# The four products of a column block of w_out with phi, emitted as one group of four strips

## The chip, the cores and the metric

The kernel runs on one core of one Trainium2 chip. The metric is device microseconds (us) of one execution of the whole program. Before the change the median of 3 runs is 520.47 us, the lowest 518.27 and the highest 520.8.

## The reference

A chain of an attention read, a gated feed-forward layer and a soft mixture of experts. Cut to what matters here:

```python
# x [8, 8, 512, 64], state [8, 8, 32, 64]; attn_out: reads of state by x and of x by state
x = attn_out.transpose(0, 2, 1, 3).reshape(8 * 544, 512)
h = x @ w_in                                   # w_in [512, 2048], held in float64
g = where(h >= 1, h, where(h <= -1, 0, (h + 1) ** 2 / 4))
x = g @ w_out                                  # w_out [2048, 512], held in float64
logits = x @ phi                               # phi [512, 32]
d = softmax of logits over the tokens; c = softmax of logits over the slots
slot_input = d.T @ x
# eight experts: relu(slot_input[e] @ w1[e]) @ w2[e]  -> slot_out
out = c @ slot_out
```

## The kernel before, in words

The feed-forward output x = g @ w_out is never formed. The kernel forms the small matrix wp = w_out @ phi (2048 by 32) once, and for each batch b = 0..7 (512 tokens each, and a ninth round for the state rows) the logits E = g @ wp. The sum d.T @ g is kept over the batches in `acc`, and multiplied by w_out only at the end.

**Conversion.** w_in and w_out lie in memory as 64-bit floats. `convert` (L155 to L171) turns a piece of 128 partitions by 512 numbers into 32-bit floats by bit operations: two on VectorE (L159, L161), and then either one more on VectorE (L164), or two on ScalarE through `act` (L133) and one on VectorE (L171). `piece` (L173) picks the one or the other by the list `CFG["conv"]`.

**w_out.** `conv_wo(i)`, i = 8..15, treats half of a block g = 0..3 of 512 rows of w_out, which lie as columns (w_out is loaded transposed): two pieces k of 128 of the 512 inner numbers each. For each piece it converts into `cw_w[k]`, which is a quarter of the tile `acc`; multiplies it by phi into the strip of partitions 32k to 32k+31 of the PSUM tile `wps[g]` (L195: the stationary operand is phi's 128 by 32, the moving one 128 by 512); turns it back by four transposes on TensorE (L198, tile `wtp`); and copies the result to `wD` on ScalarE. Behind the second half, `wD` goes to memory (L202), `wps` is copied to `wsb` on ScalarE (L204), four small products with a constant (L207) add the four strips and turn them, and ScalarE copies the result to `wp` (L208). The pool psE of `wps` has one buffer, so a block's first product waits until the block before it has been copied out at L208. `cw_w[k]` has one buffer too: the next block's piece k, whose first instruction is L159, waits until the product and the transposes that read it are done.

**Where it stands.** In the loop over b and over m = 0..15 (a step m is one `hstep`, 128 of the 2048 columns of h), `CFG["todo"]` puts the conversions into round b = 0: block 0 ahead of step m = 7, block 1 at m = 10, block 2 at m = 11, block 3 at m = 12 and 13. Each `hstep` is six products (L445; for the first four steps two, L436), two or three passes on ScalarE and GpSimd, and one on VectorE (L497). `vchunk` (tile `V`, L376) makes a quarter of the state side of h for a round: eight products side by side, then ScalarE, then a subtraction on VectorE (L395). `attention(b + 1)` runs beside it.

**What sets the order.** The program is written in this order, but up to round 2 the compiler's list scheduler places the instructions of each engine: it goes by the order in which they were emitted and by its own estimate of when operands are ready. From round 2 TensorE runs in the written order. Each engine runs its own queue in order. The helper `group` (L122) emits products that are to run side by side: the first one can be told to wait for a list of instructions, and the rest are raised in priority and ordered behind the first:

```python
first = mm(**calls[0])
for i in after:
    tc.add_manual_dep(first.ins, i.ins.name, SYNC, reason="side by side")
with tc.high_priority(CFG["hp"]):
    for c in calls[1:]:
```

It records its first product at L124 and the others at L129; `estep` (tile `E`) uses it for four strips of the same shape as those of L195.

Of the kernel before, what the change touches and what calls it, by code (L numbers as in the profile page):

```python
# [11 lines left out]
ALU = mybir.AluOpType  # L12
# [9 lines left out]
def kernel(  # L22
# [14 lines left out]
    nc = tc.nc  # L37
# [25 lines left out]
    phi_t = const.tile([128, 4, 32], F32, name="phi_t")  # L63
# [53 lines left out]
    mm = nc.tensor.matmul  # L117
# [4 lines left out]
    def group(calls, after=()):  # L122
# [6 lines that stand above are left out]
                e = mm(**c)  # L129
                tc.add_manual_dep(e.ins, first.ins.name, ORDER, reason="side by side")  # L130

    def act(out, in_, func=ACTF.Copy, **kw):
        return nc.scalar.activation(out=out, in_=in_, func=func, **kw)  # L133


    stage = [wb_s[0], wb_s[1], a_st, nat_s[3], gD_s[0], gD_s[1]] * 2 + [wb_s[0], wb_s[1], gD_s[0], gD_s[1]]
    cw_w = [acc[:, 512 * i:512 * i + 512] for i in range(4)]
# [3 lines left out]
    def stage_load(i):  # L141
        if i >= 16:
            return
        src = win[i // 2, :, 1024 * (i % 2):1024 * (i % 2) + 1024] if i < 8 else wout[i - 8]
        dma(out=stage[i].bitcast(U32), in_=src.bitcast(U32))
# [5 lines left out]
    def nxt(i):  # L151
        later = [j for j in range(i + 1, 16) if stage[j] is stage[i]]
        return later[0] if later else 16

    def convert(src, dst, tmp):  # L155

        w = src.bitcast(U32).rearrange("p (f w) -> p f w", w=2)
        lo, hi, d = w[:, :, 0], w[:, :, 1], dst.bitcast(U32)
        nc.vector.tensor_scalar(out=d, in0=hi, scalar1=0x07FFFFFF, scalar2=3,  # L159
                                op0=ALU.bitwise_and, op1=ALU.logical_shift_left)  # L160
        nc.vector.scalar_tensor_tensor(out=d, in0=hi, scalar=0xC0000000, in1=d,  # L161
                                       op0=ALU.bitwise_and, op1=ALU.bitwise_or)
        if tmp is None:
            nc.vector.scalar_tensor_tensor(out=d, in0=lo, scalar=29, in1=d,  # L164
                                           op0=ALU.logical_shift_right, op1=ALU.bitwise_or)
        else:
            t = tmp.bitcast(U32)

            act(tmp, lo, ACTF.Relu, scale=-2.0 ** -29, bias=seven)
            act(t, tmp, ACTF.Relu, scale=-1.0, bias=seven)  # L170
            nc.vector.tensor_tensor(out=d, in0=d, in1=t, op=ALU.bitwise_or)  # L171

    def piece(i, k, dst):  # L173
        rot["t"] += 1
        tmp = None if rot["t"] in CFG["conv"] else cw_t[rot["t"] % 3]
        convert(stage[i][:, 1024 * k:1024 * k + 1024], dst, tmp)

    def conv_win(i):
        c, h = divmod(i, 2)
        for k in range(2):  # L180
            piece(i, k, win_t[c][:, 2 * h + k, :])
        stage_load(nxt(i))

    wps, wD = {}, {}

    def conv_wo(i):

        g, h = divmod(i - 8, 2)
        if h == 0:
            wps[g] = psE.tile([128, 512], F32, tag="E", name="wps")  # L190
            wD[g] = rot_g.tile([128, 4, 512], F32, tag="g", name="wD")
        for k in range(2 * h, 2 * h + 2):
            w = cw_w[k]
            piece(i, k % 2, w)
            mm(out=wps[g][32 * k:32 * k + 32, :], lhsT=phi_t[:, k, :], rhs=w, start=True, stop=True)  # L195
            tp = psX.tile([128, 4, 128], F32, tag="X", name="wtp")
            for x in range(4):
                nc.tensor.transpose(tp[:, x, :], w[:, 128 * x:128 * x + 128], ident)  # L198
            act(wD[g][:, :, 128 * k:128 * k + 128], tp)
        stage_load(nxt(i))  # L200
        if h == 1:
            dma(out=wo32[g], in_=wD[g].rearrange("p x d -> p (x d)"))  # L202
            sb = rot_q.tile([128, 512], F32, tag="q", name="wsb")
            act(sb, wps[g])  # L204
            wpp = wps[g][:, 0:128].rearrange("p (x n) -> p x n", x=4)
            for x in range(4):
                mm(out=wpp[:, x, :], lhsT=sb[:, 128 * x:128 * x + 128], rhs=R4, start=True, stop=True)  # L207
            act(wp[:, 4 * g:4 * g + 4, :], wpp)  # L208
# [587 lines left out]
    drain(v0)  # L796
    drain(a0)
    todo = [lambda i=i: conv_win(i) for i in range(2, 8)] + [lambda i=i: conv_wo(i) for i in range(8, 16)]

    sm = None  # L800
    vg = None
    order = ExitStack()
    for b in range(B + 1):
# [11 lines left out]
        for m in range(NM):  # L815
# [9 lines left out]
            if b > 0 and m % 4 == 0:  # L825
                k = 4 * b + m // 4 - 2
# [102 lines left out]
    for i in range(4):  # L929
        for jj in range(4):  # L930
            mm(out=SI[32 * jj:32 * jj + 32, :], lhsT=PT[:, jj, 32 * i:32 * i + 32],
               rhs=where["wo", i][1][jj], start=(i == 0), stop=(i == 3))
# [13 lines left out]
    for i in range(16):  # L946
        e, hf = divmod(i, 2)
        place, w = where["w1", i]
        for kt in range(4):
            mm(out=h1[hf][32 * kt:32 * kt + 32, :], lhsT=XD[e // 4][:, kt, 32 * (e % 4):32 * (e % 4) + 32], rhs=w[kt],  # L950
               start=(e == 0), stop=(e == 7))
# [134 lines left out]
```

## Time and profile before

| | us |
|---|---|
| median of 3 runs | 520.47 |
| profiled execution | 520.69 |
| its span, first to last instruction | 518.5 |
| PE busy (matmul) | 462.9 |
| DVE busy | 369.0 |
| ACT busy | 313.4 |
| POOL busy | 209.5 |

PE is TensorE, PEld its weight loads, DVE is VectorE, ACT is ScalarE, POOL is GpSimd, SP issues DMAs. Every float32 product leaves two matmul records, so the 16 products of L195 are counted as 32. In a list in order of time, a row gives start, length, engine, line, operation, tiles (output <- input), and how many records are merged into it; in brackets stands how long the engine was idle before it and what ended that. Lengths overlap a little, since an instruction is counted until its last result is written; the distance from start to start is what an instruction takes from its engine.

### The profile page before, as it was taken

The numbers are of one execution on the slowest core, as the hardware profiler recorded it, in microseconds if no ns is written. First come the engines' busy times: TensorE is split into PE (matmuls) and PEld (weight loads), VectorE is DVE, ScalarE is ACT, GpSimd is POOL, SyncE is SP. The second block draws the span as 40 slices with busy tenths as digits, with TensorE's granted clock in tenths as the row PEclk, the third lists the DMA queues.
The fourth block names the chain that finished last, engine by engine and source line by source line (L and its number), as shares of the span: only waits on it lengthen the run. The fifth ranks groups of instructions, "written<-read, shape, count | busy, mean of one in ns | idle before, by whom it ended". The sixth has DMA issues, their size and how long they took to land.

```text
span 518.5 us, 9979 instructions
## 1 busy us (share of the span) xinstructions
PE 462.9 (89%) x3757; PEld 267.5 (52%) x3757; DVE 369.0 (71%) x768; ACT 313.4 (60%) x613; POOL 209.5 (40%) x211
## 2 busy tenths in 40 slices
PE   5382999999989999999998998999999769799994
PEld 2130465566545555555565455556457548335583
DVE  2999798869568879969968987985896745310370
ACT  0778997677667667767766866866656426211242
POOL 0000000045527776776776776877573100110041
PEclk9685999999999999999999999999999979989965
DMA  8998072546449797697596877789589898899998
GB/s 314 420 419 362 6 317 84 164 163 181 145 163 332 268 292 247 205 322 253 197 314 201 283 265 239 274 284 336 185 277 353 322 398 323 301 385 418 385 298 292
DMA packets 40127, 142.39 MB, mean 275 GB/s; under 512 B 3984, under 2 KB 12560, under 8 KB 27920
## 3 DMA queue, kind: packets, MB, share of 16 engines
q1 hardware_dynamic: 38400, 133.91, 72.5%
q0 software_dynamic: 1680, 7.87, 4.4%
q8 instruction: 29, 0.48, 0.4%
q14 instruction: 18, 0.15, 0.1%
HBM read 100.34 MB, written 41.42 MB: 273 GB/s over the span
## 4 chain that ended last, share of the span: by engine, by line
PE 62%; DVE 11%; DMA 7%; POOL 7%; issue 6%; ACT 5%; SPq 1%; ACTq 0%; POOLq 0%
PE h L445 24%; DMA gdr<-gD 5%; POOL v L393 4%; PE E L124 4%; PE V L124 4%; PE F L124 3%; PE h L950 3%; POOL c L475 3%; PE ops L129 3%; PE h L453 3%; PE wps L195 2%; DVE g L497 2%; ACT c L133 2%; PE gtp L523 2%; PE wtp L198 2%
## 5 line engine op out<-in xcount | busy, mean ns | idle before, releaser
L445 PE MATMUL h<-a,v 128*128 128x512 f32 x744 | 192.4, 403 | 7.1 <-DVE g L497 7.0
L445 PEld LDWEIGHTS h<-a,v 128*128 128x128 f32 x744 | 133.6, 188 | 71.2 <-DVE g L497 20.0
L475 POOL TENSOR_TENSOR c<-c 128x512 f32<-128x512 f32 x84 | 87.1, 1043 | 118.4 <-ACT c L133 117.7
L133 ACT ACTIVATE c<-h,half 128x512 f32<-128x512 f32 x128 | 87.9, 688 | 47.8 <-PE h L445 29.6
L497 DVE SCALAR_TENSOR_TENSOR g<-h,c 128x512 f32<-128x512 f32 x112 | 74.7, 671 | 36.3 <-POOL c L475 30.3
L393 POOL TENSOR_TENSOR v<-vc,v 128x512 fp32r<-128x512 f32 x48 | 61.9, 1290 | 49.6 <-ACT vc L133 49.4
L534 DVE STREAM_TRANSPOSE gD<-g 128x512 f32<-128x512 f32 x108 | 74.9, 700 | 1.8
L133 ACT ACTIVATE v<-V 128x512 fp32r<-128x512 f32 x62 | 37.1, 598 | 11.9 <-PE V L129 10.6
L124 PE MATMUL V<-win,st_t 64*32 64x512 f32 x64 | 35.9, 643 | 6.8 <-ACT att L133 5.5
L129 PE MATMUL V<-win,st_t 64*32 64x512 f32 x448 | 39.1, 636 | 0.0
L133 ACT ACTIVATE vc<-V 128x512 f32<-128x512 f32 x48 | 28.6, 596 | 15.0 <-POOL v L393 15.0
L124 PE MATMUL F<-nat,dN 128*32 128x512 f32 x54 | 26.6, 614 | 7.0 <-DMA nat<-gdr 6.6
L129 PE MATMUL E<-g,wp 128*32 128x512 f32 x168 | 29.6, 605 | 0.0
L124 PE MATMUL E<-g,wp 128*32 128x512 f32 x56 | 29.3, 605 | 0.0
L133 ACT ACTIVATE c<-c 128x512 f32<-128x512 f32 x44 | 27.8, 632 | 0.7
L129 PE MATMUL F<-nat,dN 128*32 128x512 f32 x162 | 26.8, 615 | 0.0
L453 PE MATMUL h<-XSh,v 128*128 128x256 f32 x128 | 26.1, 294 | 0.2 <-ACT nat L133 0.2
L641 DVE SCALAR_TENSOR_TENSOR acc<-acc,al,F 128x512 f32<-128x512 f32 x28 | 19.4, 724 | 7.3 <-PE F L129 7.3
L453 PEld LDWEIGHTS h<-XSh,v 128*128 128x128 f32 x128 | 20.7, 192 | 4.9 <-issue 1.7
L1036 POOL DMA_DIRECT2D out_dram<-o x16 | 7.9, 500 | 36.3 <-DVE o L1004 30.2
L129 PE MATMUL ops<-so,LC 32*128 32x256 f32 x160 | 20.6, 371 | 0.9 <-ACT o L133 0.8
L133 ACT ACTIVATE o<-ops 128x256 f32<-128x256 f32 x34 | 11.5, 381 | 15.8 <-PE ops L129 15.8
(238 smaller groups left out, 817.7 us busy)
## 6 DMA issues: line engine op xcount, KB each, us to landing
gdr<-gD SPq DMA_DIRECT2D x108, 256.0 KB, 6.8
nat<-gdr SPq DMA_DIRECT2D x27, 1024.0 KB, 6.2
w<-in_w_dram SPq DMA_DIRECT2D x24, 1024.0 KB, 10.7
xn<-in_xn_dram SPq DMA_DIRECT2D x8, 1024.0 KB, 8.6
out_dram<-o SPq DMA_DIRECT2D x16, 512.0 KB, 4.4
xs<-in_xs_dram SPq DMA_DIRECT2D x7, 1024.0 KB, 8.7
w<-in_w_dram POOLq DMA_DIRECT2D x5, 1024.0 KB, 8.9
wb<-in_win_dram SPq DMA_DIRECT2D x4, 1024.0 KB, 11.4
```

The lines of the kernel that those rows point to most:

```text
L124: first = mm(**calls[0])
L129: e = mm(**c)
L133: return nc.scalar.activation(out=out, in_=in_, func=func, **kw)
L195: mm(out=wps[g][32 * k:32 * k + 32, :], lhsT=phi_t[:, k, :], rhs=w, start=True, stop=True)
L393: nc.gpsimd.tensor_tensor(out=lo[:, G, :], in0=vf, in1=hi[:, G, :], op=ALU.subtract)
L445: mm(out=h, lhsT=v[:, G, f], rhs=a[:, G, :], start=(k == 0), stop=(k == 5))
L453: mm(out=h, lhsT=w[:, j, :], rhs=x[:, j, :], start=(k == 0), stop=(k == 11))
L475: nc.gpsimd.tensor_tensor(out=c, in0=c, in1=c, op=ALU.mult)
L497: gI[b, m] = nc.vector.scalar_tensor_tensor(out=g, in0=h, scalar=1.0, in1=c, op0=ALU.max, op1=ALU.min)
L534: nc.vector.transpose(out=gd[:, :, :, m4, :].rearrange("p c a i -> p a c i"), in_=gT[b, m].rearrange("p (a c i) -> p a c i", a=4, i=32))
L641: nc.vector.scalar_tensor_tensor(out=a, in0=a, scalar=al, in1=F, op0=ALU.mult, op1=ALU.add)
L950: mm(out=h1[hf][32 * kt:32 * kt + 32, :], lhsT=XD[e // 4][:, kt, 32 * (e % 4):32 * (e % 4) + 32], rhs=w[kt], start=(e == 0), stop=(e == 7))
```

## The change

`convert` and `piece` return the last instruction of a conversion. `conv_wo` keeps it in `cvt[k]`, no longer emits a product behind each piece, and emits the four products of a block as one `group` behind both halves, whose first product waits for the four conversions.

```diff
+            return nc.vector.scalar_tensor_tensor(out=d, in0=lo, scalar=29, in1=d, ...
+            return nc.vector.tensor_tensor(out=d, in0=d, in1=t, op=ALU.bitwise_or)
...
-        convert(stage[i][:, 1024 * k:1024 * k + 1024], dst, tmp)
+        return convert(stage[i][:, 1024 * k:1024 * k + 1024], dst, tmp)
...
-    wps, wD = {}, {}
+    wps, wD, cvt = {}, {}, {}
...
         for k in range(2 * h, 2 * h + 2):
             w = cw_w[k]
-            piece(i, k % 2, w)
-            mm(out=wps[g][32 * k:32 * k + 32, :], lhsT=phi_t[:, k, :], rhs=w, start=True, stop=True)
+            cvt[k] = piece(i, k % 2, w)
             tp = psX.tile([128, 4, 128], F32, tag="X", name="wtp")
             for x in range(4):
                 nc.tensor.transpose(tp[:, x, :], w[:, 128 * x:128 * x + 128], ident)
             act(wD[g][:, :, 128 * k:128 * k + 128], tp)
         stage_load(nxt(i))
         if h == 1:
+            group([dict(out=wps[g][32 * k:32 * k + 32, :], lhsT=phi_t[:, k, :], rhs=cw_w[k], start=True, stop=True) for k in range(4)],
+                  [cvt[k] for k in range(4)])
             dma(out=wo32[g], in_=wD[g].rearrange("p x d -> p (x d)"))
```

## Rows read from the trace of the kernel before

**Rows 1.** Busy time of each engine by stretch (us: span, engines, granted clock, DMA)
```profile
52.00:62.00 10.00, 10.00 (x50) 4.66 (x48) 6.42 (x12) 9.26 (x17) 0.00 (x0) 0.90 0.01 2
62.00:86.00 24.00, 24.00 (x158) 15.03 (x156) 23.96 (x52) 20.46 (x40) 0.00 (x0) 1.00 0.56 219
86.00:104.00 18.00, 18.00 (x158) 9.37 (x151) 13.53 (x24) 13.34 (x28) 0.00 (x0) 1.00 0.39 118
52.00:107.20 55.20, 55.20 (x383) 31.83 (x389) 43.95 (x87) 45.86 (x88) 1.10 (x2) 0.98 0.40 146
107.20:400.00 292.80, 282.93 (x2249) 160.76 (x2234) 238.37 (x471) 198.43 (x382) 194.62 (x183) 1.00 0.76 251
```

**Rows 2.** The same by stretch, of line 195 alone (PE, PEld, clock, DMA)
```profile
52.00:62.00 10.00, 2.73 (x8) 0.42 (x8) 0.90 0.01 2
62.00:86.00 24.00, 4.28 (x12) 0.56 (x10) 1.00 0.56 219
86.00:104.00 18.00, 6.28 (x14) 0.83 (x14) 1.00 0.39 118
```

**Rows 3.** PE in order of time: single products, and two at once
```profile
55.45 1.04 PE L195 MATMUL wps<-acc,phi_t 128*32 128x512 f32 x2
56.42 0.44 PE L198 MATMUL wtp<-cst_t,acc 128*128 128x128 f32 x2
...
58.40 1.04 PE L195 MATMUL wps<-acc,phi_t 128*32 128x512 f32 x2
...
61.37 1.05 PE L195 MATMUL wps<-acc,phi_t 128*32 128x512 f32 x4
```

**Rows 4.** PE in order of time: four strips of the tile E, one group
```profile
121.10 0.63 PE L129 MATMUL E<-g,wp 128*32 128x512 f32 x3
...
121.56 0.60 PE L129 MATMUL E<-g,wp 128*32 128x512 f32 x3
```

**Rows 5.** DVE in order of time: ends of blocks 0 to 2, starts of blocks 1 to 3
```profile
53.74 0.69 DVE L171 TENSOR_TENSOR acc<-acc,LT 128x512 uint32<-128x512 uint32 x1 [0.84 <-ACT LT L133]
58.61 0.42 DVE L159 TENSOR_SCALAR acc<-gD 128x512 uint32<-128x512 uint32 x1
73.03 0.68 DVE L164 SCALAR_TENSOR_TENSOR acc<-gD,acc 128x512 uint32<-128x512 uint32 x1
74.37 0.43 DVE L159 TENSOR_SCALAR acc<-wb 128x512 uint32<-128x512 uint32 x1
85.07 0.43 DVE L159 TENSOR_SCALAR acc<-gD 128x512 uint32<-128x512 uint32 x1
85.41 0.70 DVE L164 SCALAR_TENSOR_TENSOR acc<-wb,acc 128x512 uint32<-128x512 uint32 x1
```

**Rows 6.** DVE in order of time: its waits of the same stretch
```profile
61.47 0.43 DVE L159 TENSOR_SCALAR acc<-gD 128x512 uint32<-128x512 uint32 x1 [0.99 <-PE wtp L198]
86.77 0.69 DVE L497 SCALAR_TENSOR_TENSOR nat<-h,c 128x512 f32<-128x512 f32 x1 [0.67 <-ACT c L133]
90.20 0.43 DVE L159 TENSOR_SCALAR acc<-gD 128x512 uint32<-128x512 uint32 x1 [1.14 <-PE wtp L198]
93.20 0.43 DVE L159 TENSOR_SCALAR acc<-gD 128x512 uint32<-128x512 uint32 x1 [0.77 <-PE wtp L198]
102.08 0.69 DVE L395 TENSOR_TENSOR v<-V,v 128x512 fp32r<-128x512 f32 x1 [0.66 <-ACT v L133]
```

**Rows 7.** PE in order of time: last products of blocks 2 and 3, first step of round 1
```profile
90.09 1.05 PE L195 MATMUL wps<-acc,phi_t 128*32 128x512 f32 x2
102.68 1.05 PE L195 MATMUL wps<-acc,phi_t 128*32 128x512 f32 x2
104.51 1.62 PE L445 MATMUL h<-a,v 128*128 128x512 f32 x6
```

**Rows 8.** Busy time and granted clock by stretch (columns as in rows 1)
```profile
50.00:55.00 5.00, 5.00 (x24) 1.63 (x23) 4.16 (x7) 3.03 (x5) 0.00 (x0) 0.60 0.05 21
445.00:450.00 5.00, 3.02 (x23) 1.20 (x23) 3.05 (x12) 1.50 (x6) 0.79 (x2) 1.00 0.64 225
```

More of the change, by code (lines that the diff above doesn't have):

```diff
@@ L163, in convert @@
         if tmp is None:
-            nc.vector.scalar_tensor_tensor(out=d, in0=lo, scalar=29, in1=d,
-                                           op0=ALU.logical_shift_right, op1=ALU.bitwise_or)
+            return nc.vector.scalar_tensor_tensor(out=d, in0=lo, scalar=29, in1=d,
+                                                  op0=ALU.logical_shift_right, op1=ALU.bitwise_or)
         else:
@@ L170, in convert @@
             act(t, tmp, ACTF.Relu, scale=-1.0, bias=seven)
-            nc.vector.tensor_tensor(out=d, in0=d, in1=t, op=ALU.bitwise_or)
+            return nc.vector.tensor_tensor(out=d, in0=d, in1=t, op=ALU.bitwise_or)
     def piece(i, k, dst):
```

## The prediction, on record before the changed kernel ran

> **What bounds the kernel now.** I read four views. The first is the page's row of 40 slices, to find the stretch that the change touches. The second is busy time by stretch [rows 1]: from 52 to 104 us PE has no idle time, and in the long rounds behind it (107.2 to 400 us) it is busy for 282.93 of 292.80 us. So PE is what the other engines feed from 52 us on, and time that is really taken out ahead of 104 us should stay out, since the later loads and exchanges are released by work that moves with it. The third is the same view of line 195 alone [rows 2]: 2.73, 4.28 and 6.28 us, 13.29 us in all for 16 products. The fourth is VectorE in order of time [rows 5, 6], because PE being full does not say that VectorE has room. It has little: 23.96 of 24.00 us busy from 62 to 86, against 6.42 of 10 before and 13.53 of 18 after [rows 1]. That division decides my number.
>
> **What is removed.** A single product takes PE from 55.45 to 56.42, 0.97 us, and is drawn 1.04 long; two products that happen to stand together take 1.05 [rows 3]. Four strips of the same shape in a group take from 121.10 to 121.56 + 0.60, 1.06 us [rows 4]. So a block of four costs 1.06 where it cost up to four times 1.04. Over the four blocks PE is asked for 13.29 - 4 x 1.06 = 9.05 us less. That is the ceiling. No instruction is added on any engine: 16 products, 64 transposes, copies, conversions and DMAs are the same in number and size, and the loads of the next half-block and the store of `wD` keep their place relative to conversions and transposes, so the queues of SP and POOL carry the same.
>
> **How much of it counts, by stretch.**
> From 52 to 62 us. Block 0 is fully converted at 53.74 + 0.69 = 54.43 [rows 5], before its first single product starts (55.45, [rows 3]); the group can stand where that product stood, and waits for nothing. The single at 58.40 then leaves the queue ahead of the transposes for which VectorE waits 0.99 us at 61.47 [rows 6]. VectorE starts its full stretch 0.97 us earlier. I count **1.0**.
> From 62 to 86 us. PE loses 4.28 - 1.06 = 3.2 us of work (block 1's group stays here, block 2's falls behind 86), but VectorE has 0.04 us of room [rows 1, 2]. All of this becomes idle time of PE. I count **0**. The cover that hides the gain is VectorE's own work (attention of round 1, the steps' L497 and the conversions); only if that work thinned out would the 3.2 appear.
> From 86 to 104 us. PE loses 6.28 - 2 x 1.06 = 4.2 us [rows 2]. VectorE idles 4.47, of which PE causes three pieces: 0.67 for ScalarE's `c`, which hangs on a step's products, and 1.14 and 0.77 for transposes that stand behind single products [rows 6]. Together **2.6**, less than the 4.2 that PE gives up, so I count all of it. At the end VectorE delivers the last operand of round 1 at 102.08 + 0.69 = 102.77, and PE begins that round at 104.51 [rows 6, 7]; in the 1.74 between stands the last single product, which begins at 102.68. The group can go ahead of that operand: **1.0** more. The other 0.7 is transposes, which stay.
>
> **What is added.** A wait. The group needs all four conversions of its block, and `cw_w[k]` is free for the next block's L159 only when the group has read it. Behind the group on PE stand steps and transposes, which ScalarE and VectorE wait for. Lower bound of the cost: zero for blocks 0 and 1, whose successors begin at 58.61 and 74.37 while their own conversions end at 54.43 and 73.03 + 0.68 = 73.71 [rows 5] (block 1's successor would come 0.4 late, with other work ready on a full VectorE). For block 2, L159 of block 3 starts at 85.07, before block 2's own last conversion ends at 85.41 + 0.70 = 86.11 [rows 5]. Group and all, it can't start before 86.11 + 1.06 = 87.2, 2.1 us later; in that time VectorE has a step's L497 to do [rows 6] and not much else. I take **0.5** lost. Upper bound: the groups stand where the last single product of each block stood; that is the slower rival.
>
> Sum: 1.0 + 0 + 2.6 + 1.0 - 0.5 = 4.1 us. The profiled execution took 520.69 (518.5 span and 2.19 around it), 0.22 above the median. 520.47 - 4.1 = **516.4**. Its own range, 513 to 518.5: the added wait may cost 0 to 2 more, and 3.2 from the middle stretch may be partly usable, since PE runs ahead there.
>
> **A rule that speaks against it.** In the trace, a PE with 3.02 us busy out of 5 kept a granted clock of 1.00, the 2.4 GHz level, while from 50 to 55 us, busy throughout, it was mostly at the 1.2 GHz level, 0.60 on the mean [rows 8]. The Trainium skill, "TensorE: Matmul & The Clock Gate", section "A second HAM failure mode: psum-queue depth-cycling", says that frequent small idle gaps between groups of products can make the clock swing between its two levels. By that rule the new gaps from 62 to 86 us would cost clock; by the row they would not. It is the fourth rival.
>
> **Rivals.**
> *VectorE takes it all.* PE runs ahead and waits; the 2.6 us of VectorE's idle time are refilled by waits on the group. For it: the full middle stretch [rows 1]. Against it: two of the three pieces are waits on transposes that stand right behind single products [rows 6]. Gain 0 to 1.5: about 519.8.
> *All of PE's time is carried.* The scheduler lays out the instructions anew and fills PE's room with steps. For it: VectorE has 11.25 us idle in 52 to 107.2, as 43.95 busy of 55.20 shows [rows 1]. Against: the idle time lies outside the middle. Gain 9: about 511.5.
> *The next block waits for the group (slower).* Place: L159 of the blocks 1 and 3. If the groups stand where the last single products stood, they end at 61.37 + 1.05 = 62.42 and 90.09 + 1.05 = 91.14 [rows 3, 7], against the starts of L159 at 58.61 and 85.07 [rows 5]: 3.8 and 6.1 us late. Block 2 lies inside the full stretch, where a delay is a change of order, and is left out. Of the 3.8, 0.99 was a wait already; of the 6.1, 0.67 + 1.14 were, and 1.74 is slack at the end. That leaves 2.8 + 2.5, less the 1.0 that block 1's earlier transposes still give: 4.3 us slower, 524.8. It decides once block 3 is delayed by more than 1.8 + 1.74 + 1.0 = 4.5 us. For it: block 2's last single product started 4.0 us after its conversion (90.09 against 86.11). Against: much of that delay was the queue of single products and transposes itself.
> *The clock swings.* One stretch like 50 to 55 us at 0.60 costs 5 x 0.4 = 2.0 us [rows 8]: 516.4 + 2.0 = 518.4.
> That the strips do not run side by side I leave out: the group of the tile E has the same shape and does [rows 4].
>
> **How the numbers follow.** Chances: forecast 0.50, VectorE takes it all 0.17, all carried 0.11, slower 0.17, clock 0.05. A measurement of this kernel can tell about 0.5% (2.6 us) from no change, so faster means below 517.9 and slower above 523.1. Faster: 0.43 of the first, 0.11, 0.01: 0.55. Same: 0.07 of the first, 0.16, 0.04 of the clock, 0.01 of the slower one: 0.28. Slower: 0.16 and 0.01 of a bad layout with no gain: 0.17. Range 511 to 523.5: it takes in the case with all carried and the near half of the slower one, and leaves out some 0.05 below and 0.12 above.
>
> **What would show it.** Right: four rows of products of `wps` with four strips side by side of about 1.06 us; the first of them near 55.5; PE idle a few us between 62 and 86 while VectorE stays full; the waits at 90.20 and 93.20 gone; the first step of round 1 on PE near 100.5 and everything behind it earlier by the same. Wrong: VectorE idle ahead of an L159 with a product of `wps` as its releaser, above all at block 3; PE idle ahead of a group; the clock below 1.00 between 62 and 104; or a gain ahead of 104 us that is gone again before 400.

## The result, and the profile after

| | before | after |
|---|---|---|
| median of 20 runs each, side by side | 519.37 | 526.19 |
| lowest and highest | 513.01, 522.28 | 520.24, 530.78 |
| profiled execution | 520.69 | 520.24 |

The changed kernel is slower: the ratio is 1.012, with a 95% interval from 1.0092 to 1.0148. The forecast was 516.4 and faster. The medians differ by 6.8 us, and 526.19 lies above the end of the range, 523.5. Ratios here are taken over the runs within 1.5% of the fastest of their kernel in the same job, so that one very fast run narrows what is kept, and a ratio can differ from the quotient of two medians.

The profiled execution after is the lowest of its 20 runs, so it is 6 us short of its own median, and it must be known where. Most of it is the tail. Late in the span PE waits for `nat` to come back from memory, and this wait was the shortest that any profile here shows. One row each, PE in order of time, before, after, and a second profile of the same changed kernel:

```profile
419.05 1.03 PE L124 MATMUL F<-nat,dN 128*32 128x512 f32 x1 [6.65 <-DMA nat<-gdr]
```

```profile
420.33 0.59 PE L124 MATMUL F<-nat,dN 128*32 128x512 f32 x1 [3.05 <-DMA nat<-gdr]
```

```profile
425.40 1.03 PE L124 MATMUL F<-nat,dN 128*32 128x512 f32 x1 [7.42 <-DMA nat<-gdr]
```

The second profile's wait is 4.4 us longer, and its execution took 526.83, 6.6 more. The profile of the kernel before is in its turn 1.3 us above its median, so a delay against it reads too small by about that much.

All that follows is therefore read at places ahead of the tail. Three marks on PE serve: **M0**, the first step of `h` behind the two groups of `V` near 52 us, which stands ahead of every product of `wps`; **M1**, the last row of `S` of round 3's attention, behind which round 2's steps begin; and **M2**, the next row of 59 records of `sp`. They fall at the same point of the work in every kernel here: from M0 to M1 each has 757 or 758 records on PE.

**What the change did.** By line, PE from 52 to 107 us of the changed kernel (busy us, mean ns):

```profile
L129 PE MATMUL wps<-acc,phi_t 128*32 128x512 f32 x24 | 4.2, 605 | 0.0
L124 PE MATMUL wps<-acc,phi_t 128*32 128x512 f32 x8 | 4.2, 604 | 0.0
```

The two lines lie side by side: 4.2 us in place of the 13.29 of [rows 2]. The 9.05 us are saved as forecast. But PE did not stay full. Busy time by stretch of the changed kernel, columns as in [rows 1]:

```profile
52.00:62.00 10.00, 10.00 (x75) 5.76 (x60) 7.00 (x14) 9.77 (x19) 0.00 (x0) 0.97 0.01 2
62.00:86.00 24.00, 22.29 (x146) 15.47 (x145) 23.91 (x52) 22.72 (x45) 0.00 (x0) 1.00 0.60 219
86.00:104.00 18.00, 14.98 (x157) 9.52 (x164) 13.53 (x24) 12.58 (x27) 2.03 (x2) 0.91 0.40 129
52.00:107.20 55.20, 50.47 (x401) 33.06 (x386) 47.60 (x95) 46.60 (x89) 3.07 (x3) 0.96 0.45 159
107.20:400.00 292.80, 278.79 (x2186) 156.54 (x2186) 231.97 (x458) 193.37 (x373) 191.97 (x180) 0.99 0.75 246
```

PE idles 1.71 us from 62 to 86 and 3.02 from 86 to 104, 4.73 in all, where it idled 0.00 before [rows 1]. The last row is the second surprise: PE is busy 4.1 us less behind 107.2 us, too. VectorE in order of time, the start of block 3, the last operand and the first `g` of round 1:

```profile
87.44 1.11 DVE L159 TENSOR_SCALAR acc<-gD 128x512 uint32<-128x512 uint32 x3 [1.52 <-PE wps L129]
...
98.99 0.70 DVE L396 TENSOR_TENSOR v<-V,v 128x512 fp32r<-128x512 f32 x1
102.68 0.69 DVE L498 SCALAR_TENSOR_TENSOR g<-h,c 128x512 f32<-128x512 f32 x1 [2.99 <-POOL c L476]
```

PE in order of time, from M0 to M2:

```profile
53.12 1.66 PE L446 MATMUL h<-a,v 128*128 128x512 f32 x6
...
86.82 0.60 PE L129 MATMUL wps<-acc,phi_t 128*32 128x512 f32 x3
...
93.76 1.22 PE L446 MATMUL h<-a,v 128*128 128x512 f32 x2 [2.45 <-ACT a L133]
94.77 1.94 PE L197 MATMUL wtp<-cst_t,acc 128*128 128x128 f32 x8
...
155.61 1.09 PE L129 MATMUL S<-xs,st_t 64*32 64x512 f32 x14
...
164.55 2.29 PE L446 MATMUL h<-a,v 128*128 128x512 f32 x6 [3.52 <-DVE g L498]
166.64 1.91 PE L281 MATMUL eTp<-cst_t,att 128*128 128x128 f32 x8
...
184.63 1.01 PE L129 MATMUL sp<-xn,att 128*32 128x64 f32 x59
```

and the same marks and place in the kernel before:

```profile
53.76 1.76 PE L445 MATMUL h<-a,v 128*128 128x512 f32 x6
...
156.43 1.09 PE L129 MATMUL S<-xs,st_t 64*32 64x512 f32 x14
...
162.10 1.66 PE L445 MATMUL h<-a,v 128*128 128x512 f32 x6 [0.28 <-DVE g L497]
163.59 1.04 PE L280 MATMUL eTp<-cst_t,att 128*128 128x128 f32 x8
...
179.92 1.01 PE L129 MATMUL sp<-xn,att 128*32 128x64 f32 x59
```

PE by stretch from M0 to M1 (busy, clock, DMA), before and then after:

```profile
53.76:156.43 102.67, 100.55 (x757) 1.00 0.46 155
53.12:155.61 102.49, 95.39 (x758) 0.98 0.48 157
```

Read them as two losses. At M1 the changed kernel is 0.82 us ahead (155.61 against 156.43), but 0.64 of that stands already at M0, ahead of everything that was changed. From M0 to M1 it gains 0.2: PE is busy 5.2 us less and idle 5.0 us more. So of the 9.05 us between 0.2 and 0.8 reach M1. From M1 to M2 it takes 29.02 us against 23.49, so it loses 5.5 there, and arrives 4.7 late. Four rounds later (341.92 before, 346.78 after) it is 4.9 late: nothing grows or heals. The granted clock fell behind both long waits. PE by stretch (busy, clock, DMA):

```profile
92.00:97.00 5.00, 3.23 (x11) 0.67 0.92 323
165.00:170.00 5.00, 5.00 (x30) 0.66 0.98 410
445.00:450.00 5.00, 3.37 (x29) 1.00 0.73 301
```

**What differs between M1 and M2.** From round 2 PE has the written order, but the list scheduler still places the other engines, and with a changed round 0 it placed their entry into round 2 otherwise, 60 us behind the edit. GpSimd before, then after:

```profile
159.97 1.04 POOL L475 TENSOR_TENSOR c<-c 128x512 f32<-128x512 f32 x1 [1.76 <-ACT c L133]
160.97 2.06 POOL L270 TENSOR_TENSOR att<-att,m 128x512 f32<-128x512 f32 x2
```

```profile
159.99 2.06 POOL L271 TENSOR_TENSOR att<-att,m 128x512 f32<-128x512 f32 x2 [2.61 <-DVE nb L249]
162.00 2.04 POOL L476 TENSOR_TENSOR c<-c 128x512 f32<-128x512 f32 x2
```

ScalarE before, then after:

```profile
159.14 0.69 ACT L133 ACTIVATE c<-h,half 128x512 f32<-128x512 f32 x1 [2.76 <-PE h L445]
160.24 0.69 ACT L133 ACTIVATE att<-S,nb 128x512 f32<-128x512 f32 x1 [0.41 <-DVE nb L248]
```

```profile
159.43 0.69 ACT L133 ACTIVATE att<-S,nb 128x512 f32<-128x512 f32 x1 [3.88 <-DVE nb L249]
...
160.11 0.68 ACT L133 ACTIVATE c<-h,half 128x512 f32<-128x512 f32 x1
```

Step 0's `c` now stands behind attention's exponential on ScalarE and behind attention's two subtractions on GpSimd. Its `g` on VectorE starts at 163.82 in place of 161.36, and PE, which runs in the written order from there on, waits 3.52 us with the products of the fourth step.

### The profile page after: what moved, and what is told of

Its sections match the earlier page's. It is cut to its first block, busy times and chain, and to the rows that moved or that the text cites. A ratio compares the mean times of both kernels' runs of the same rounds, so it can differ in the third digit from the quotient of the medians.

```text
span 518.0 us, 9981 instructions
## 1 busy us (share of the span) xinstructions
PE 458.9 (89%) x3757; PEld 268.8 (52%) x3757; DVE 370.1 (71%) x768; ACT 313.3 (60%) x613; POOL 209.4 (40%) x211
## 4 chain that ended last, share of the span: by engine, by line
PE 47%; DVE 17%; DMA 13%; POOL 7%; ACT 7%; issue 7%; SPq 1%; ACTq 0%; POOLq 0%
PE h L446 20%; DMA w<-in_w_dram 6%; DMA gdr<-gD 4%; POOL v L394 4%; PE E L124 4%; PE V L124 3%; POOL c L476 3%; PE F L124 3%; PE h L454 3%; PE ops L129 2%; ACT c L133 2%; DVE g L498 2%; DMA nat<-gdr 2%; PE gtp L524 2%; DVE acc L161 1%
## 5 line engine op out<-in xcount | busy, mean ns | idle before, releaser
L124 PE MATMUL F<-nat,dN 128*32 128x512 f32 x54 | 25.7, 598 | 3.4 <-DMA nat<-gdr 3.1
L129 PE MATMUL F<-nat,dN 128*32 128x512 f32 x162 | 26.0, 598 | 0.0
L1037 POOL DMA_DIRECT2D out_dram<-o x16 | 7.9, 500 | 35.4 <-DVE o L1005 29.2
```

The costliest lines, as they stand in the source:

```text
L1037: (nc.gpsimd.dma_start if CFG["og"] else dma)(out=out[544 * bb + 512:544 * bb + 544, dc], in_=o[32 * q:32 * q + 32, t, :])
```

## The experiments

Four theories were put to them. **A**: the other order at the entry of round 2 makes the loss. **B**: PE's new idle time in round 0 makes it. **C**: the tail makes it. **D**: VectorE is what PE waits for once its products are grouped, so PE's saved time turns into waiting and into clock.

All runs in one table. A difference is that of the medians, to the kernel before in the same job (519.46, 519.17, 519.63 and 519.68 in the four jobs); the ratio, with its 95% interval, is to the same. PE is its busy time from 52 to 104 us, 52.00 in the kernel before.

| kernel | median (runs) | difference | ratio | PE | M0 to M1 | M1 | M2 | M1 to M2 |
|---|---|---|---|---|---|---|---|---|
| before | 519.37 (20) | | | 52.00 | 102.67 | 156.43 | 179.92 | 23.5 |
| after | 526.19 (20) | +6.8 | 1.012 (1.0092 to 1.0148) | 47.27 | 102.49 | 155.61 | 184.63 | 29.0 |
| after, again | 525.99 (6) | +6.5 | 1.0102 (1.0062 to 1.0142) | 46.97 | 102.69 | 156.25 | 185.32 | 29.1 |
| after, order mended | 523.64 (12) | +4.2 | 1.0039 (1.0 to 1.0078) | 45.91 | 105.52 | 157.80 | 182.52 | 24.7 |
| before, order reversed | 524.39 (10) | +4.9 | 1.0095 (1.0062 to 1.0128) | 52.00 | 102.60 | 155.84 | 185.08 | 29.2 |
| blocks 0 to 2 grouped | 521.05 (12) | +1.9 | 1.0097 (1.0048 to 1.0147) | 46.85 | 102.82 | 155.53 | 178.98 | 23.5 |
| block 3 grouped | 526.56 (6) | +7.4 | 1.0172 (1.0095 to 1.0249) | 51.90 | 101.77 | 155.44 | 185.50 | 30.1 |
| blocks 0, 1 grouped | 518.48 (12) | -1.2 | 1.0001 (0.9972 to 1.0029) | 50.40 | 100.77 | 153.87 | 177.31 | 23.4 |
| order mended, light | 515.23 (12) | -3.9 | 0.9978 (0.9934 to 1.0022) | 49.55 | 96.36 | 147.87 | 172.59 | 24.7 |
| before, light | 517.10 (12) | -2.1 | 0.9838 (0.9759 to 0.9918) | 52.00 | 101.08 | 152.67 | 176.14 | 23.5 |
| after, filler | 525.82 (6) | +6.2 | 1.0125 (1.0089 to 1.0161) | 46.91 | 103.97 | 157.14 | 184.66 | 27.5 |
| half groups, order mended | 517.64 (12) | -2.0 | 0.9967 (0.9943 to 0.999) | 50.91 | 99.22 | 153.12 | 177.86 | 24.7 |
| the same again | 518.26 (12) | -1.4 | 1.0058 (0.9993 to 1.0122) | 50.45 | 99.65 | 152.34 | 177.06 | 24.7 |
| half groups | 521.91 (6) | +2.2 | 1.0143 (1.0028 to 1.0257) | 50.84 | 99.30 | 152.20 | 181.27 | 29.1 |

**The changed kernel again.** No edit.

> The changed kernel once more, for a second profile beside its times. Theory A (order): the change saves PE its 9 us, but the list scheduler, given other times, also places step 0 of round 2 on ScalarE and GpSimd behind the attention of round 3; PE waits 3.5 us there and works at a lower clock behind it, about 5.6 us lost in all. A expects 524 to 528 us and the same wait of 3 to 4 us before the second step of round 2. Theory B (PE's new idle time): what is lost is the idle time of PE ahead of 104 us (4.7 us, one wait of 2.45 us for round 1's first step), and the entry of round 2 only shows it. B expects the same time. Theory C (tail): the first rounds don't matter, the weights' DMAs of the last 120 us set the end, and they run slower here. C expects a trace that differs from the first one in the last 120 us and not ahead of it.

M1 to M2 took 29.1 us and PE waited 3.55 at 165.19: the loss is the kernel's, not one execution's. Its tail wait is the 7.42 shown above. That the tail can be 3.05 or 7.42 in one and the same kernel speaks against theory C.

**The order alone.** Two order edges (which carry no semaphore) put step 0 of round 2 ahead of the exponential and the subtractions of round 3's attention in the changed kernel, and behind it in the kernel before:

```diff
-                act(e2[G], S[G], ACTF.Exp, ...)
+                behind(act(e2[G], S[G], ACTF.Exp, ...), b, "act", 0)
...
-                (nc.gpsimd if ...).tensor_tensor(out=t3, ..., op=ALU.subtract)
+                behind((nc.gpsimd if ...).tensor_tensor(out=t3, ..., op=ALU.subtract), b, "pool", 0)
```

where `behind(i, b, engine, m)` orders `i` of b = 3 behind (or, for the reverse, ahead of) the instruction of step m of round 2 that `hstep` recorded on that engine.

> The changed kernel with two order edges: the first exponential of round 3's attention on ScalarE and its subtractions on GpSimd stand behind step 0 of round 2, as in the kernel before. Everything ahead of it is as in the changed kernel. A: the 3.5 us wait at the second step of round 2 is below 1 us, the stretch from the first step of round 2 to the state read near 180 us is 5 us shorter than in the changed kernel, and the time is 518 to 520.5 us, 5 to 7 below the changed kernel. B: no change against the changed kernel, 524 to 527. C: no change, 524 to 527.

> The kernel before, single products and all, with the same two edges turned round: step 0 of round 2 stands behind the exponential on ScalarE and the subtractions on GpSimd. PE and SP have the order of the kernel before throughout. A: slower than before by 4 to 6 us, 523.5 to 525.5, with a wait of about 3.5 us on PE at the second step of round 2 and a granted clock below 1.00 behind it. B: as before, 519 to 520, since PE's idle time ahead of 104 us is not there. C: as before.

Reversed, the kernel before became 4.9 us slower, as A expected; its instructions have the order of before on all four engines up to M1, and PE is full there. PE in order of time of that kernel:

```profile
155.84 1.09 PE L129 MATMUL S<-xs,st_t 64*32 64x512 f32 x14
156.86 4.37 PE L453 MATMUL h<-a,v 128*128 128x512 f32 x18
164.95 2.51 PE L453 MATMUL h<-a,v 128*128 128x512 f32 x6 [3.72 <-DVE g L505]
```

It is the changed kernel's wait, at the same place. So A is shown, at about 4.9 us, and B falls as the only cause. Mended, the changed kernel had 24.7 us between M1 and M2 and a wait of 0.68, but its median was 523.64, where A expected 518 to 520.5: only 2.4 us came back of 525.99, and its ratio is hardly clear of 1. Two things stand against the rest. The two edges don't restore the old order whole: from M1 to M2 1.2 us more remain than before. And M1 came 2.2 us later than in the changed kernel, though the order of instructions up to there is the same on all four engines. The delay arises between 95 and 100 us, where the clock differs. PE by stretch (busy, clock, DMA), in the changed and then in the mended kernel:

```profile
98.00:100.00 2.00, 2.00 (x11) 1.00 0.00 0
```

```profile
98.00:100.00 2.00, 2.00 (x7) 0.50 0.00 0
```

So the order isn't all, and grouping itself can cost in round 0. One profile does not say how much of it a typical execution pays.

**Which block.** The group only for the blocks named, single products for the rest:

```diff
+            if g not in (0, 1, 2):
+                mm(out=wps[g][32 * k:32 * k + 32, :], lhsT=phi_t[:, k, :], rhs=w, start=True, stop=True)
...
-            group([...], [cvt[k] for k in range(4)])
+            if g in (0, 1, 2):
+                group([...], [cvt[k] for k in range(4)])
```

> Blocks 0, 1 and 2 as groups, block 3 by single products; no order edges (step 0 of round 2 stands first by itself here). Theory A (order at the entry of round 2): no wait of 3.5 us there, so no 5 us loss; PE is asked for about 6.5 us less. If only A were at work, 513 to 516 us. Theory D (PE's saved time turns into waiting ahead of 104 us because VectorE is full, and a drop of the clock behind the wait takes some of the rest): 518 to 521, level with the kernel before, with PE idle 3 to 5 us between 62 and 104.

> Block 3 alone as a group, the others by single products. Its list order at the entry of round 2 is that of the changed kernel (attention ahead of step 0). A: the 3.5 us wait and the lower clock are there though only one block is grouped: 522.5 to 525. D alone: 518 to 519.5, since PE stays full ahead of 104 us.

> Blocks 0 and 1 as groups, 2 and 3 by single products; no order edges, step 0 of round 2 stands first by itself. PE is asked for about 4 us less, most of it in the stretch where VectorE is full. D: PE idles 2 to 3 us between 62 and 86 us; the time is 517.5 to 519.5, level with the kernel before or up to 2 us faster. Order alone (theory A): 515 to 516.

Block 3 alone, at most 4 x 1.04 - 1.06 = 3.1 us of PE's work less and PE all but full, gave the bad entry of round 2 and the whole loss (526.56, above A's range too); so the flip doesn't hang on the size of the edit. The kernels with blocks 0 to 2 and 0 and 1 kept the order of before by themselves (23.5 and 23.4 from M1 to M2), so they show what grouping does without it. With block 2 in the group, VectorE and PE in order of time:

```profile
87.81 1.10 DVE L159 TENSOR_SCALAR acc<-gD 128x512 uint32<-128x512 uint32 x3 [1.51 <-PE wps L129]
```

```profile
94.11 0.73 PE L449 MATMUL h<-a,v 128*128 128x512 f32 x2 [2.44 <-ACT a L133]
```

These are the changed kernel's 1.52 and 2.45. Both are in every kernel here that groups block 2 as four with all of VectorE's work in it, and in none that doesn't. With blocks 0 and 1 only, M1 comes 2.6 us earlier than before, 1.9 of them from M0 on; grouping block 2 as well takes 1.7 of that away (2.0 from M0 on), with a clock of 1.00 from M0 to M1 in both. The 1.9 us by which the median with blocks 0 to 2 is slower stand in no trace: its profile, at 518.71, is 2.3 below its own median.

**Is it VectorE?** The conversions of w_out without their second VectorE operation (L161), 16 operations of some 0.6 us, in the mended and in the kernel before (edges that keep its own order). The part left out is the sign and top exponent bit of w_out.

```diff
-        nc.vector.scalar_tensor_tensor(out=d, in0=hi, scalar=0xC0000000, in1=d, ...)
+        if sign:
+            nc.vector.scalar_tensor_tensor(out=d, in0=hi, scalar=0xC0000000, in1=d, ...)
```

> The run with the groups and step 0 first (a_ord), with one of three VectorE instructions left out of each of the 16 conversions of w_out (L161: the sign is not copied), 16 x 0.6 = 9.6 us less for VectorE. D: VectorE is what PE waits for, so PE's idle time ahead of 104 us shrinks by 3 us or more, the wait for round 1's first step with it, and the time falls by 4 to 8 us below a_ord: 515 to 519. If PE or the tail were the bound (theories B and C): within 1.5 us of a_ord.

> The kernel before with the same instruction left out of the same 16 conversions and the order edges that it has by itself. D: PE has no idle time ahead of 104 us there, so VectorE's 9.6 us are worth 0 to 2 us: 517.5 to 520. If VectorE were the bound of both kernels, it would gain as a_light does.

M1 came 9.9 us earlier in the mended kernel (157.80 to 147.87) and 3.8 in the kernel before (156.43 to 152.67), but 2.2 of these 3.8 are there at M0 (53.76 to 51.59), ahead of which PE still waits for VectorE (9.53 us until 48.16 before, 8.33 until 46.59 light). From M0 to M1 the gains are 9.2 and 1.6. PE by stretch, mended, then mended and light:

```profile
52.00:104.00 52.00, 45.91 (x346) 31.01 (x339) 43.00 (x85) 43.27 (x84) 0.21 (x1) 0.93 0.40 142
```

```profile
52.00:104.00 52.00, 49.55 (x417) 32.13 (x416) 45.81 (x96) 46.96 (x94) 7.18 (x7) 1.00 0.48 183
```

The 2.45 wait is gone and the clock is whole. Some of the 9.2 is that clock (0.93 in this profile of the mended kernel, with the filler's the lowest of all); against the changed kernel's own 102.49 the gain is 6.1, still nearly four times that of the kernel before. At the medians it is 8.1 against 2.1, across two jobs for the first; the ratios do not serve here, since that of the kernel before, light, rests on two of its 12 runs (507.24 and 510.07, the others from 516.03 up). So D is borne out: grouped, PE waits for what VectorE delivers; with single products it is in the main PE's own work that bounds. No edge held the order of rounds 0 and 1 here or where blocks were chosen, so what a new layout adds to these numbers is not shown.

**What the clock costs.** Twelve small products of a constant with itself, in PE's wait at the entry of round 2 of the changed kernel, order untouched:

```diff
+            if b == 2 and m == 2:
+                fill = psV.tile([128, 128], F32, tag="V", name="fill")
+                for _ in range(12):
+                    mm(out=fill, lhsT=ident, rhs=ident, start=True, stop=True)
```

> The changed kernel with 12 small products of a constant with itself, about 3.1 us of PE time at the higher clock level, put between the third and the fourth step of round 2, into the wait of 3.5 us; their result isn't used. No other instruction of any engine changes its place. If the clock behind the wait is part of what the entry of round 2 costs (h, eTp and E of about 4.5 us of PE time took 6 us there), the granted clock stays at 1.00, the stretch to the state read near 184 us is 1.3 to 1.8 us shorter, and the time is 524 to 525 against 526. If the clock is no part of it: 526 to 526.5, or more where the products reach past the wait.

```profile
162.41 2.84 PE L851 MATMUL fill<-cst_t 128*128 128x128 f32 x24
166.09 1.69 PE L446 MATMUL h<-a,v 128*128 128x512 f32 x6 [0.84 <-DVE g L498]
167.61 1.03 PE L281 MATMUL eTp<-cst_t,att 128*128 128x128 f32 x8
```

Behind the filler the step took 1.69 us, not 2.29, and the eight transposes 1.03, not 1.91. M1 to M2 fell from 29.0 to 27.5. So 1.5 of the 5.5 us lost there is clock and the other 4 are waits: 3.2 more at the fourth step (3.52 against 0.28), and 0.75 between the seventh and the eighth, which start at 173.90 and 176.17 after and at 169.88 and 171.40 before. The median hardly moved, and in this profile M0 to M1 took 1.5 us longer than in the changed kernel's, its clock 0.93 from 52 to 104 us: a miss as a mend, good as a measurement.

**A version that keeps the saving.** Groups of two strips, one behind each half block, so that `cw_w[0]` and `cw_w[1]` come free half a block earlier; with the two edges, and without:

```diff
+            if k % 2:
+                group([dict(out=wps[g][32 * q:32 * q + 32, :], ...) for q in (k - 1, k)],
+                      [cvt[q] for q in (k - 1, k)])
```

> Groups of two strips per half block in place of four per block, and step 0 of round 2 first (the order edges of a_ord). PE is asked for about 5 us less than before, and a block's first half is read before its second is converted. Theory D (PE's time turns into waiting on VectorE): PE idles less ahead of 104 us than with groups of four (1 to 3 us against 4.7), and the time is 517 to 520. If waiting for the whole block were the main loss, it would be 515 to 517.

> The same kernel as a_half, on another chip and beside a_half0: if its gain is real and not of that one chip, 516 to 519.5, 1 to 3 us ahead of the kernel before, and PE near full from 52 to 104 us.

> Groups of two strips, one behind each half block, without the two order edges of a_half; the list scheduler by itself then puts GpSimd's subtractions of the attention of round 3 ahead of step 0 of round 2, as in the changed kernel. Theory A (the order at the entry of round 2 costs about 5 us whatever the conversions look like): PE waits some 3.5 us for VectorE's g near 160-165 us, the state-read row of round 2 comes 4 to 6 us later than in a_half (177.86 us), and the time is 521.5 to 524. Rival D alone (what VectorE leaves PE sets the time, the order is a bystander): the same as a_half within 1.5, 516.5 to 519.

A pair takes PE as long as a group of four, so 8.4 us in all and 4.9 saved. The wait at L159 for a group is gone and PE is busy for 50.91 of 52.00. From M0 to M1 3.0 to 3.5 us of it are kept. With the edges the ratio was 0.9967 (0.9943 to 0.999) and M2 came 2.1 us earlier than before; on the second chip the medians were 1.4 apart in the same direction, but the ratio, 1.0058 (0.9993 to 1.0122), doesn't confirm it. Without the edges the scheduler chose the bad order again, M1 to M2 was 29.1 with a wait of 3.52 at 161.14, and the median was 3.65 above that of the same kernel with them, whose order up to M1 is the same: theory A once more, under another round 0.

## Why the prediction was wrong

*The saving of PE* (13.29 to 4 x 1.06): right. The four groups run side by side and cost 4.2; the first begins at 56.98, not near 55.5.

*That VectorE sets the pace, and where it idles:* right as a reading. PE idled between 62 and 86 while VectorE was full for 23.91 of 24.00, the waits at 90.20 and 93.20 of [rows 6] went, and the first `g` of round 1 came at 102.68, 4.5 us earlier than before (107.17): almost the 4.1 forecast. VectorE's last operand of round 1 was done at 98.99 + 0.70, 3.1 us earlier than before, which is 1.0 + 2.6 - 0.5; but that is in part luck, since by 86 us VectorE had done only 0.5 us more work (30.91 busy from 52 on, 30.38 before), and the new wait was 1.5.

*The step that failed first:* "time that is really taken out ahead of 104 us should stay out". The 4.1 us were counted on VectorE's milestone, but up to M1 PE is the engine that carries the time: it was busy for 42.98 of 43.00 us from 104 to 147 before, and for 42.38 after. At M1 PE was 0.8 us ahead in place of 4.1, and from M0 to M1 it gained 0.2 (102.67 to 102.49), in the second profile nothing (102.69). The account from M0 to M1: it was asked for 9.05 less, but its busy time fell by 5.2, since `h`, `F`, `E`, `wtp`, `sp` and `gtp` were 3.1 longer for the same records, at a lower clock or less close together, and 0.8 is overlap of lengths; its idle time grew by 5.0. Time that is taken out stayed out only as far as the other engines kept PE fed.

*The added wait, priced at 0.5:* mis-sized, and the place was right. L159 of block 3 was forecast 2.1 us late and came 2.4 late (85.07 to 87.44). VectorE waited 1.52 us for the group there, then had its conversions in a heap, and PE stood 2.45 us until 93.76, for ScalarE's `a` of round 1's attention. With it, grouping block 2 made M1 later by 1.7 us and not earlier (153.87 to 155.53, blocks 0 and 1 against blocks 0 to 2), and where the low clock behind the wait lasted longest, M1 came 2.2 us later again (157.80 against 155.61). It is the mechanism of the slower rival; the rival's own price, 4.3, was not measured apart.

*What was priced at nearly nothing:* that the order of other instructions would change 60 us later. The prediction has a new layout only as a gain (all of PE's time carried) and as "a bad layout with no gain" at 0.01. The list scheduler re-placed the entry of round 2 on three engines, for 4.9 us as the reversal shows, which is the larger part of the loss. The medians do not split it sharply: 6.8 less 4.9 leaves 1.9, as much as blocks 0 to 2 grouped in the good order cost, but mending the order gave back 2.4 only, and block 3 alone, in the bad order and with PE all but full, cost 7.4. The slower rival's number, 524.8, came near by luck: mostly for another reason.

*The clock:* a rival at 0.05, and it occurred as a part, behind the long waits. The short waits, 0.38 to 0.76 us, that came from 62 to 86 left it at 1.00. The Trainium skill, "TensorE: Matmul & The Clock Gate", section "HAM oscillation — how this bites in real kernels", says that a wait for a DMA between two stretches of products, where it is long enough, lets the next stretch start at the lower clock. The trace agrees behind the waits of 3.52 (0.66) and 2.45 (0.67), which were waits for other engines, but the same 2.44 us in the kernel with blocks 0 to 2 grouped was followed by 1.00 from 92 to 97 and from 95 to 100 us.

Open stays what in the scheduler's estimates tips the order: grouping block 3 or half groups tip it, grouping blocks 0 to 2 or 0 and 1 does not, and no run looked inside. Open is also what a typical execution of the mended kernel pays in round 0.

## What to carry to other kernels

Where a list scheduler places instructions, an edit's effect has two parts, the edit and the new order; compare the order of every engine, also rounds later, and pin the order (or reverse it in the old kernel) before blaming the edit. Time taken from a full engine is worth only what its feeders can keep up with, and it must be counted on the engine that carries the path, not on a milestone of another. A group that waits for its last operand also holds all buffers of its first: the smaller group, with half the saving, was the better one, by 2.0 and 1.4 us at the medians of two chips and only once clear of no change.

## What the hardware showed

Behind a wait of about 2.45 us on PE the clock fell from its 2.4 GHz level to the 1.2 GHz one for a part of the time. The changed kernel, its second profile, the filler's and the mended one have the same order of instructions up to M1, and yet the low clock lasted differently: from 98 to 100 us the clock was 1.00, 1.00, 0.50 and 0.50, and M0 to M1 took 102.49, 102.69, 103.97 and 105.52 us (the same 16 records of `h` took 3.90 in the changed kernel and 5.82 in the mended one). With blocks 0 to 2 grouped it was 1.00 throughout. The kernel before and its reversal, with PE full, took 102.67 and 102.60. Two strips side by side cost PE what four do (1.05 us). Twelve 128 by 128 products fitted into a 3.5 us wait and the clock was 1.00 behind it, from 165 to 170 us, where it was 0.66 without them.
